# The last 96 hidden columns and the gate column computed with x stationary, turned by a transposing DMA

## The chip, the cores and the metric

The kernel runs on one core of one Trainium2 chip. It is a program for five engines that run side by side and meet only at semaphores: TensorE (PE, matmuls; PEld is its loading of weights), VectorE (DVE), ScalarE (ACT), GpSimd (POOL), and SyncE (SP), which here only issues DMAs. The metric is the device time of one execution in microseconds (us); the median of three runs is given.

## The reference

With x of 2048 tokens by 512, in bf16:

```python
g = sigmoid((x * gate_w).sum(-1))                 # one gate per token
a = linear_attention(x, wqkv, w_phi) @ wo         # 32 heads of 16
b = relu(x @ w1) @ w2                             # w1: 512 x 1376
return g * a + (1 - g) * b
```

In the attention branch q and k are projected per head by `w_phi`; the softmax of the result and the softmax of its negative, side by side, are the features. k features and v make one 32 x 16 matrix per head (`kv`), and each token's output is its q features times `kv`, divided by its q features times the sum of the k features. Nothing is causal: all of k and v must be done before the first output.

## The kernel before

**Tiling.** Tokens are taken in four chunks of 512 (index c or a) and 16 tiles of 128 (index m). x is kept transposed in `XT` (features on the partitions). `W1` has 1376 columns in eleven tiles of 128 (index k); the last tile has only 96 (`KREM`), and the gate weights are loaded as column 1376 beside it, so that the gate logits come out of the same matmuls.

**The hidden layer.** For each chunk and column tile, `pe_h` (line 394) makes four matmuls over the 512 features, with W1's columns stationary and 512 tokens moving. The result has the hidden columns on the partitions and the tokens along the row, which is the layout that the second layer needs as its stationary operand. ACT's Relu (`rl{a}_{k}`, line 460) copies it from PSUM to `HT`. For the last column tile (k = 10) 97 partitions come out: 96 hidden columns and, on partition 96, the 512 gate logits of the chunk.

**The gate.** DVE clamps this one row (`gr`, line 464), a DMA writes it to a scratch tensor in DRAM (`g1`, line 435), and a second DMA reads it back so that each token is on a partition of its own (`g2`, line 438). ACT makes the exponential (`ge`) and adds one (`gp`), DVE takes the reciprocal (`go`): 1 - g is 1/(1 + e), and g is e/(1 + e). `EG` scales the attention branch (line 615), `OMG` the output (line 679).

**The attention branch.** `v` (line 480) and the projections `pr` (line 499, with `w_phi` folded into the weights first, `pe_fold`, line 372) run on PE between the hidden tiles; maximum, minimum, sum and reciprocal run on DVE, subtractions and scalings on POOL, exponentials on ACT. `kv` (line 560) gathers k features and v on PE. For q, a transposing DMA per tile turns the features (`tq`, line 582), `nd` (line 604) multiplies them with `kv`, DVE divides (`rd`, `o`), and a second transposing DMA turns the result (`to`, line 620).

**The output.** `b{m}` (line 625) multiplies a tile of `HT` with `W2`, `a{m}` (line 632) adds the turned attention output times `wo` into the same PSUM bank; ACT scales and copies (`oe`), and a store follows (`st`).

**What sets the order.** Each engine's whole order of work is written out by hand in `ORDER` at the top, one list of step names per engine. An engine goes through its list strictly in order and waits at each step for the semaphores of what the step needs. SP's list is therefore also the order in which its DMAs are issued. PSUM has eight banks; the hidden tiles take turns in banks 3, 4 and 5 (`HB`), and a bank is free again when what is in `freed` is done, for the last column tile the Relu and the clamp.

Of the kernel before, what the change touches and what calls it, by code (L numbers as in the profile page):

```python
# [5 lines left out]
ACT = mybir.ActivationFunctionType  # L6
# [9 lines left out]

ORDER = {
# [4 lines left out]
    ),  # L22
    "pool": (
# [125 lines left out]
def bass_gated_mix__linear_kernel_hedgehog__dense_activation_relu__prompt_kernel(  # L149
# [13 lines left out]
    S, D = x2.shape  # L163
# [24 lines left out]
    with ExitStack() as es:  # L188
        E = es.enter_context

        def sb(name, shape, dt):
            return E(nc.sbuf_tensor(name, shape, dt))
# [31 lines left out]
        ROWM = sb("ROWM", [P, GH], I32)  # L224
        GB = sb("GB", [P, P], FP32)
        MK = sb("MK", [P, GH], FP32)
        GROW = sb("GROW", [P, 2, 512], FP32)
        GL = sb("GL", [P, NT], FP32)
        EG = sb("EG", [P, NT], FP32)
        EP = sb("EP", [P, NT], FP32)  # L230
        OMG = sb("OMG", [P, NT], FP32)
        PS = E(nc.psum_tensor("PS", [P, 8, 512], FP32))
        GSCR = nc.dram_tensor("gate_scratch", [S], FP32)
        EPS = 8 * 512

        def ap(t, row, off, dims):
            return bass.AP(tensor=t, offset=off, ap=[[row, P]] + [list(d) for d in dims])

        def psap(off, dims):
            return ap(PS, EPS, off, dims)  # L240
# [8 lines left out]
            boost=700.0)  # L249
        add("ones", "pool", lambda q: q.memset(  # L250
            ap(VS, NT * NG * GZ, GV, [[GZ, NT * NG], [1, 1]]), 1.0), dur=0.7, boost=-1e4)
        XN = FT[:, NF - 2, :].rearrange("p (m d) -> p m d", d=D)
        one = nc.const_aps.tensor(1.0, (P, 1), BF16).tensor
        ones_w, ones_m = (bass.AP(tensor=one, offset=0, ap=[[1, P], [0, n]]) for n in (P, 512))
# [26 lines left out]
        def chunk(c):  # L281
            return slice(c * 512, (c + 1) * 512)
# [109 lines left out]
        w1of = {k: (() if k < 4 else ("w1b",) if k < 8 else ("w1c",)) for k in range(KT)}  # L392

        def pe_h(q, c, k, b):
            m = P if k < KT - 1 else KREM + 1
            for j in range(ND):
                last = q.matmul(PS[0:m, b, :], W1[:, j, k * P:k * P + m], XT[:, j, chunk(c)],  # L397
                                start=(j == 0), stop=(j == ND - 1))
            return last

        def pe_h_first(q, j, c0, c1):
# [30 lines left out]
        def gate(c):  # L432

            s4 = slice(4 * c, 4 * c + 4)
            add(f"g1_{c}", "sp", lambda q, c=c: q.dma_start(out=GSCR[chunk(c)].rearrange("(o n) -> o n", o=1),
                                                             in_=GROW[KREM:KREM + 1, c % 2, :]),
                (f"gr{c}",), dur=0.1, lat=2.0, dma=True)
            add(f"g2_{c}", "sp", lambda q, c=c, s4=s4: q.dma_start(
                out=GL[:, s4], in_=GSCR[chunk(c)].rearrange("(m p) -> p m", p=P),
                allow_slow_non_contiguous=True),  # L440
                (f"g1_{c}",), dur=0.2, lat=3.0, dma=True)
            add(f"ge{c}", "act", lambda q, s4=s4: q.activation(EG[:, s4], GL[:, s4], ACT.Exp), (f"g2_{c}",), dur=0.22)
            add(f"gp{c}", "act", lambda q, s4=s4: q.activation(EP[:, s4], EG[:, s4], ACT.Copy, bias=1.0), (f"ge{c}",),
                dur=0.2)
            add(f"go{c}", "dve", lambda q, s4=s4: q.reciprocal(OMG[:, s4], EP[:, s4]), (f"gp{c}",), dur=0.15)

        for n, (kind, a, k) in enumerate(units):
            b = GB4[n] if n < 4 else HB[(n - 4) % len(HB)]
            if kind == "h":
                rows = P if k < KT - 1 else KREM  # L450
                halved = n < 4
                deps = [*xof[a], *w1of[k], prev, *freed[b]]
                if k == KT - 1:
                    deps.append("gw")
                add(f"h{a}_{k}", "pe", lambda q, a=a, k=k, b=b, h=halved:
                    pe_h_rest(q, k, (3 if k < 2 else 2) * P, 4 * P, k > 1) if h else pe_h(q, a, k, b),
                    deps, dur=(0.22 if k < 2 else 0.44) if halved else 0.87,
                    boost=8000.0 if n < 3 else 0.0)
                prev = f"h{a}_{k}"
                add(f"rl{a}_{k}", "act", lambda q, a=a, k=k, b=b, rows=rows: q.activation(  # L460
                    HT[0:rows, k, chunk(a)], PS[0:rows, b, :], ACT.Relu), (prev,), dur=0.6, boost=RL)
                freed[b] = (f"rl{a}_{k}",)
                if k == KT - 1:
                    add(f"gr{a}", "dve", lambda q, a=a, b=b: q.tensor_scalar(
                        GROW[KREM:KREM + 1, a % 2, :], PS[KREM:KREM + 1, b, :], GATE_LIMIT, -GATE_LIMIT,
                        ALU.min, ALU.max), (prev, f"rl{a}_{k}", f"g1_{a - 2}" if a > 1 else None), dur=0.69, boost=500.0)
                    freed[b] += (f"gr{a}",)
                    gate(a)
            else:
                deps = ["wqT", *wbd, prev, *freed[b]]  # L470
                add(f"f{a}_{k}", "pe", lambda q, a=a, k=k, b=b: pe_fold(q, a, k, b), deps, dur=0.24, boost=1000.0)
                prev = f"f{a}_{k}"
                evict(f"fe{a}_{k}", FE, WP[:, a, k, :], b, (prev,), boost=1000.0)
                freed[b] = (f"fe{a}_{k}",)
# [32 lines left out]
        for jn, (kind, tiles) in enumerate(jobs):  # L507
# [61 lines left out]
            else:  # L569
# [29 lines left out]
                for m in tiles:  # L599
# [39 lines left out]
                    if m == NT - 1:  # L639

                        hb = (ab, 0)
                        cols = [slice(0, 352), slice(352, D)]
                        last_b = f"b{m}"

                        def pe_bh(q, m=m, hb=hb, cols=cols):
                            for b, cs in zip(hb, cols):
                                for k in range(KT):
                                    r = P if k < KT - 1 else KREM
                                    last = q.matmul(PS[:, b, 0:cs.stop - cs.start], HT[0:r, k, m * P:(m + 1) * P], W2[0:r, k, cs],  # L649
                                                    start=(k == 0), stop=False)  # L650
                            return last

                        g.add(last_b, "pe", pe_bh, ("w2a", "w2b", *(f"rl{m // 4}_{k}" for k in range(KT)), *war,
                                                    f"ev_{J}"), dur=2.42)
                        for h2 in range(2):
                            b, cs = hb[h2], cols[h2]

                            def pe_ah(q, m=m, b=b, cs=cs):
                                for t in range(ND):
                                    last = q.matmul(PS[:, b, 0:cs.stop - cs.start], OT[:, m % NOT, t, :], WO[:, t, cs],  # L660
                                                    start=False, stop=(t == ND - 1))
                                return last

                            add(f"a{m}_{h2}", "pe", pe_ah, (last_b, "wo", f"to{m}", f"a{m}_0" if h2 else None), dur=0.44)
                            need = (f"a{m}_{h2}", f"go{m // 4}", f"st{m - NOS}")
                            if h2 == 0:
                                add(f"oe{m}_0", "act", lambda q, m=m, b=b, cs=cs: q.activation(
                                    OSB[:, m % NOS, cs], PS[:, b, 0:cs.stop - cs.start], ACT.Copy, scale=OMG[:, m:m + 1]), need, dur=0.45)
                            else:
                                add(f"oe{m}_1", "dve", lambda q, m=m, b=b, cs=cs: q.tensor_scalar(  # L670
                                    OSB[:, m % NOS, cs], PS[:, b, 0:cs.stop - cs.start], OMG[:, m:m + 1], None, ALU.mult), need,
                                    dur=0.4)
                            add(f"st{m}_{h2}", ("act", "sp")[h2], lambda q, m=m, cs=cs: q.dma_start(
                                out=o2[m * P:(m + 1) * P, cs], in_=OSB[:, m % NOS, cs]), (f"oe{m}_{h2}",), dur=0.5,
                                lat=1.5, dma=True)
                        continue
                    g.add(f"b{m}", "pe", pe_b, ("w2a", "w2b", *(f"rl{m // 4}_{k}" for k in range(KT)), *war), dur=2.38)
                    add(f"a{m}", "pe", pe_a, (f"b{m}", "wo", f"to{m}"), dur=0.87)
                    add(f"oe{m}", "act", lambda q, m=m, ab=ab: q.activation(  # L679
                        OSB[:, m % NOS, :], PS[:, ab, :], ACT.Copy, scale=OMG[:, m:m + 1]),  # L680
# [66 lines left out]
```

## Time and profile before

| | |
|---|---|
| Time, median of 3 runs | 151.53 us (151.14, 151.53, 152.31) |
| The profiled execution: span | 150.2 us, 2515 instructions |
| Median less that span | 1.33 us |
| PE / DVE / ACT / POOL busy | 145.2 / 113.4 / 92.2 / 109.4 us |
| Clamp of the gate row (DVE, 1x512) | 4 times 697 ns |
| Tail Relu (ACT, 96x512) | 4 times 599 ns |
| Transposing DMA of an attention tile (128x512) | 16, median 2.4 us from issue to landing |
| Gate read back from DRAM | 4, median 3.7 us from issue to landing |

All other times come from the one profiled execution, whose first instruction of the program is at 0 and whose last ends at 150.2. For that execution only the span is given; what a run takes beyond it lies around the program's instructions. The page gives the busy time of each engine, the span in 40 slices of 3.75 us each (a digit is the busy share in tenths), the chain of work that ended last, the groups of instructions by line, and the DMA issues. A group row ends with busy time, mean duration of one, and idle time before. Matmuls overlap one another, so the mean duration of one (379 ns for 512 columns) is longer than the distance from one to the next (216 ns), which is read from the chain: four in 0.86 us.

### The profile page before, as it was taken

To read this page: it belongs to the slowest core of one execution; us is meant where nothing else is said; L and a number is where in the kernel's file an instruction comes from. 1 tells how busy PE (TensorE), PEld (TensorE's weight loads), DVE (VectorE), ACT (ScalarE), POOL (GpSimd) and SP (SyncE) were. 2 spreads that over 40 slices of the span, in tenths; PEclk is the share of its full clock that TensorE was granted. 3 is DMA by queue.
4 is the path that set the end of the run, shared out by engine and by line. 5 is a ranking of instruction groups with operands and counts; after the bars stand their busy time and mean duration, and the time that the engine had idled before them with its cause. 6 is when DMAs were issued, how large, how long until landed. Compare 5 with 4: busy or idle time off the path is not lost.

```text
span 150.2 us, 2515 instructions
## 1 busy us (share of the span) xinstructions
PE 145.2 (97%) x944; PEld 74.2 (49%) x961; DVE 113.4 (76%) x168; ACT 92.2 (61%) x127; POOL 109.4 (73%) x71
## 2 busy tenths in 40 slices
PE   7899999999999999999999999999999999999992
PEld 3664444445554465445444545445444454454461
DVE  2433666999899949979999899999999969436301
ACT  3356769799969766698983937446546551310151
POOL 3000499999999999999999999998999791330000
PEclk9999999999999999999999999999999999999999
DMA  4999995000005602300000230476698774986251
GB/s 146 280 179 233 213 203 108 0 0 0 7 1 132 218 4 66 103 0 0 4 0 0 56 86 18 92 175 140 174 110 173 179 209 105 109 212 140 64 162 53
DMA packets 46307, 15.59 MB, mean 104 GB/s; under 512 B 39796, under 2 KB 46292, under 8 KB 46296
## 3 DMA queue, kind: packets, MB, share of 16 engines
q1 hardware_dynamic: 43560, 12.99, 42.0%
q10 hardware_dynamic: 2736, 2.45, 5.1%
q8 instruction: 7, 0.11, 0.4%
q14 instruction: 4, 0.03, 0.1%
HBM read 4.42 MB, written 2.11 MB: 43 GB/s over the span
## 4 chain that ended last, share of the span: by engine, by line
PE 93%; DMA 3%; issue 1%; ACT 1%; SPq 1%; DVE 0%
PE PS L628 24%; PE PS L397 23%; PE PS L502 18%; PE PS L482 9%; PE PS L634 9%; PE PS L563 3%; PE PS L606 3%; DMA W<-in_B_w_dram 3%; PE PS L649 2%; PE PS L374 1%; ACT HT L460 1%; PE PS L403 1%; PE PS L660 1%; SPq L272 1%; PE PS L409 0%
## 5 line engine op out<-in xcount | busy, mean ns | idle before, releaser
L542 POOL TENSOR_TENSOR TS<-PB,MX 128x1024 bf16<-128x1024 bf16 (+1 forms) x18 | 30.9, 1723 | 14.9 <-DVE MX L533 14.9
L397 PE MATMUL PS<-XT,W 128*128 128x512 bf16 (+1 forms) x156 | 38.3, 379 | 0.2
L628 PE MATMUL PS<-W,HT 128*128 128x512 bf16 (+1 forms) x160 | 37.5, 379 | 0.3
L549 DVE TENSOR_REDUCE ZB<-FT 128x128 f32<-128x2048 bf16 (+1 forms) x18 | 36.6, 2031 | 1.0 <-ACT FT L547 1.0
L547 ACT ACTIVATE FT<-TS 128x2048 bf16<-128x2048 bf16 (+1 forms) x18 | 30.9, 1718 | 7.7 <-POOL TS L542 7.5
L542 POOL TENSOR_TENSOR TS<-MN,PB 128x1024 bf16<-128x1024 bf16 (+1 forms) x18 | 30.9, 1724 | 0.8 <-DVE MN L535 0.8
L502 PE MATMUL PS<-WP,XT 128*128 128x512 bf16 x124 | 30.0, 379 | 0.2
L556 POOL TENSOR_TENSOR FT<-FT,SC 128x2048 bf16<-128x2048 bf16 (+1 forms) x9 | 29.5, 3290 | 0.0
L460 ACT ACTIVATE HT<-PS 128x512 bf16<-128x512 f32 (+1 forms) x44 | 24.7, 597 | 5.8 <-PE PS L397 4.9
L628 PEld LDWEIGHTS PS<-W,HT 128*128 128x128 bf16 (+1 forms) x165 | 15.5, 98 | 17.1
L533 DVE TENSOR_REDUCE MX<-PB 128x64 bf16<-128x1024 bf16 (+1 forms) x18 | 19.5, 1085 | 5.8 <-ACT PB L529 5.7
L397 PEld LDWEIGHTS PS<-XT,W 128*128 128x128 bf16 (+1 forms) x160 | 15.6, 101 | 16.5
L679 ACT ACTIVATE OSB<-PS,OMG 128x512 bf16<-128x512 f32 x15 | 10.2, 687 | 20.3 <-PE PS L634 20.3
L535 DVE TENSOR_REDUCE MN<-PB 128x64 bf16<-128x1024 bf16 (+1 forms) x18 | 19.3, 1084 | 2.3 <-ACT PB L529 2.3
L529 ACT ACTIVATE PB<-PS 128x1024 bf16<-128x1024 f32 (+1 forms) x18 | 16.7, 927 | 6.7 <-PE PS L502 3.8
L502 PEld LDWEIGHTS PS<-WP,XT 128*128 128x128 bf16 x128 | 12.1, 98 | 13.9 <-DVE WP L344 0.4
L579 POOL TENSOR_TENSOR FT<-FT,SR 128x1024 bf16<-128x1024 bf16 (+1 forms) x9 | 15.6, 1739 | 0.7
L482 PE MATMUL PS<-WV,XT 128*128 128x512 bf16 x62 | 16.0, 379 | 0.1
L634 PE MATMUL PS<-WO,OT 128*128 128x512 bf16 x58 | 14.2, 378 | 0.1
L615 DVE SCALAR_TENSOR_TENSOR OTM<-PS,EG,RD 128x256 bf16<-128x256 f32 x32 | 13.8, 463 | 0.2
L613 DVE RECIPROCAL RD<-PS 128x16 f32<-128x16 f32 x32 | 6.5, 235 | 9.0 <-PE PS L606 8.8
L491 ACT ACTIVATE VS<-PS 128x512 bf16<-128x512 f32 x16 | 9.6, 603 | 4.8 <-PE PS L482 4.7
(50 smaller groups left out, 97.8 us busy)
## 6 DMA issues: line engine op xcount, KB each, us to landing
out_dram<-OSB ACTq DMA_DIRECT2D x15, 128.0 KB, 2.1
W<-in_B_w_dram SPq DMA_DIRECT2D x1, 1280.0 KB, 6.7
W<-in_B_w_dram SPq DMA_DIRECT2D x1, 512.0 KB, 5.6
WV<-in_A_wqkv_dram SPq DMA_DIRECT2D x1, 512.0 KB, 4.7
WO<-in_A_wo_dram SPq DMA_DIRECT2D x1, 512.0 KB, 4.7
FT<-in_A_x_dram SPq DMA_DIRECT2D x3, 128.0 KB, 4.0
W<-in_B_w_dram SPq DMA_DIRECT2D x1, 352.0 KB, 3.9
W<-in_B_w_dram ACTq DMA_DIRECT2D x2, 128.0 KB, 3.7
```

Of the source, the lines that this page charges most:

```text
L397: last = q.matmul(PS[0:m, b, :], W1[:, j, k * P:k * P + m], XT[:, j, chunk(c)], start=(j == 0), stop=(j == ND - 1))
L460: add(f"rl{a}_{k}", "act", lambda q, a=a, k=k, b=b, rows=rows: q.activation(HT[0:rows, k, chunk(a)], PS[0:rows, b, :], ACT.Relu), (prev,), ...
L482: last = q.matmul(PS[:, 2, :], XT[:, j, m * P:(m + 1) * P], WV[:, j, :], start=(j == 0), stop=(j == ND - 1))
L502: last = q.matmul(PS[:, n, :], XT[:, j, m * P:(m + 1) * P], WP[:, s, j, :], start=(j == 0), stop=(j == ND - 1))
L533: add(f"mx_{J}", "dve", lambda q, sl=sl, w=w, i=pbg: q.tensor_reduce(MX[:, sl, 0:w * H], i, AX.X, ALU.max), (f"ev_{J}", old("t1")), dur=0. ...
L535: add(f"mn_{J}", "dve", lambda q, sl=sl, w=w, i=pbg: q.tensor_reduce(MN[:, sl, 0:w * H], i, AX.X, ALU.min), (f"ev_{J}", old("t2")), dur=0. ...
L542: add(f"{tn}_{J}", "pool", lambda q, o3=o3, a3=a3, b3=b3: q.tensor_tensor(o3, a3, b3, ALU.subtract), (f"{'mx' if sg == 0 else 'mn'}_{J}", ...
L547: add(f"ex_{J}", "act", lambda q, fs=fs, ts=ts, w=w: q.activation(FT[:, fs, 0:w * F], TS[:, ts, 0:w * F], ACT.Exp), (f"t1_{J}", f"t2_{J}", ...
L549: add(f"sm_{J}", "dve", lambda q, fs=fs, sl=sl, w=w: q.tensor_reduce(ZB[:, sl, 0:2 * w * H], FT[:, fs, 0:w * F].rearrange("p (g d) -> p g ...
L556: add(f"nm_{J}", "pool", lambda q, f3=f3, sl=sl, w=w: q.tensor_tensor(f3, f3, SC[:, sl, 0:2 * w * H].unsqueeze(2).to_broadcast([P, 2 * w * ...
L628: last = q.matmul(PS[:, ab, :], HT[0:r, k, m * P:(m + 1) * P], W2[0:r, k, :], start=(k == 0), stop=False)
L634: last = q.matmul(PS[:, ab, :], OT[:, m % NOT, t, :], WO[:, t, :], start=False, stop=(t == ND - 1))
```

## The change

For the last column tile the operands change places. `pe_h_tail` makes four groups of four matmuls per chunk: 128 tokens of x stationary, the 97 columns of W1 (with the gate column) moving. The result has tokens on the partitions and, for each of the four token tiles, 97 values along the row. The Relu copies 4 x 96 of these to a new tile `HR`, whose rows are padded to 128 columns with zeros once at the start (`hpad`, on POOL). A transposing DMA `hx{a}` on SP's queue turns `HR` into the place of the tail in `HT`; the output step `b{m}` now waits for it. The gate logits are already one token per partition: the clamp reads four values per partition from PSUM straight into `GL`, and `g1`, `g2`, `GROW` and the DRAM scratch are gone.

```diff
     "sp": (
-        "... x3 gw g1_1 g2_1 w2a g1_0 g1_2 w2b wo g2_0 tq0 tq1 "
-        "g1_3 to0 tq2 tq3 to1 tq4 tq5 to2 to3 tq6 to4 tq7 g2_3 to5 g2_2 tq8 to6 ..."
+        "... x3 gw w2a w2b wo hx0 hx1 hx2 tq0 tq1 "
+        "hx3 to0 tq2 tq3 to1 tq4 tq5 to2 to3 tq6 to4 tq7 to5 tq8 to6 ..."
     "pool": (
-        "iota_r iota_i iota_c ones t1_k0 ..."
+        "iota_r iota_i iota_c ones hpad t1_k0 ..."
...
-        GROW = sb("GROW", [P, 2, 512], FP32)
+        HR = sb("HR", [P, 2, 4, P], BF16)
...
-        GSCR = nc.dram_tensor("gate_scratch", [S], FP32)
...
+        add("hpad", "pool", lambda q: q.memset(HR[:, :, :, KREM:P], 0.0), dur=0.6, boost=-1e4)
...
+        def pe_h_tail(q, c, b):
+            m = KREM + 1
+            for n in range(4):
+                for j in range(ND):
+                    last = q.matmul(PS[:, b, n * m:(n + 1) * m], XT[:, j, c * 512 + n * P:c * 512 + (n + 1) * P],
+                                    W1[:, j, (KT - 1) * P:(KT - 1) * P + m], start=(j == 0), stop=(j == ND - 1))
+            return last
...
-            add(f"g1_{c}", "sp", ...)
-            add(f"g2_{c}", "sp", ...)
-            add(f"ge{c}", "act", lambda q, s4=s4: q.activation(EG[:, s4], GL[:, s4], ACT.Exp), (f"g2_{c}",), dur=0.22)
+            add(f"ge{c}", "act", lambda q, s4=s4: q.activation(EG[:, s4], GL[:, s4], ACT.Exp), (f"gr{c}",), dur=0.22)
...
+                    add(f"h{a}_{k}", "pe", lambda q, a=a, b=b: pe_h_tail(q, a, b), deps, dur=0.69)
+                    prev = f"h{a}_{k}"
+                    hrow = psap(b * 512, [[KREM + 1, 4], [1, KREM]])
+                    add(f"rl{a}_{k}", "act", lambda q, a=a, i=hrow: q.activation(
+                        HR[:, a % 2, :, 0:KREM], i, ACT.Relu), (prev, f"hx{a - 2}" if a > 1 else None), dur=0.6, boost=RL)
+                    add(f"hx{a}", "sp", lambda q, a=a: q.dma_start_transpose(
+                        out=HT[:, KT - 1, chunk(a)].rearrange("p (n t) -> p n t", t=P),
+                        in_=HR[:, a % 2, :, :].rearrange("p n k -> p (n k)")),
+                        (f"rl{a}_{k}", "hpad"), dur=1.2, lat=1.6, dma=True)
+                    add(f"gr{a}", "dve", lambda q, a=a, b=b: q.tensor_scalar(
+                        GL[:, 4 * a:4 * a + 4], psap(b * 512 + KREM, [[KREM + 1, 4]]), GATE_LIMIT, -GATE_LIMIT,
+                        ALU.min, ALU.max), (prev, f"rl{a}_{k}"), dur=0.2, boost=500.0)
+                    freed[b] = (f"rl{a}_{k}", f"gr{a}")
...
-                    g.add(f"b{m}", "pe", pe_b, ("w2a", "w2b", *(f"rl{m // 4}_{k}" for k in range(KT)), *war), dur=2.38)
+                    g.add(f"b{m}", "pe", pe_b, ("w2a", "w2b", *(f"rl{m // 4}_{k}" for k in range(KT - 1)), f"hx{m // 4}", *war), dur=2.38)
```

The orders of PE, ACT and DVE stay as they were.

More of the change, by code (lines that the diff above doesn't have):

```diff
@@ L394, in pe_h @@
         def pe_h(q, c, k, b):
-            m = P if k < KT - 1 else KREM + 1
             for j in range(ND):
-                last = q.matmul(PS[0:m, b, :], W1[:, j, k * P:k * P + m], XT[:, j, chunk(c)],
+                last = q.matmul(PS[:, b, :], W1[:, j, k * P:(k + 1) * P], XT[:, j, chunk(c)],
                                 start=(j == 0), stop=(j == ND - 1))
+            return last
[5 more added lines that the diff above has]
+                                    W1[:, j, (KT - 1) * P:(KT - 1) * P + m], start=(j == 0), stop=(j == ND - 1))
             return last
@@ L434, in gate @@
             s4 = slice(4 * c, 4 * c + 4)
[L435 to L441, printed above, removed]
-            add(f"ge{c}", "act", lambda q, s4=s4: q.activation(EG[:, s4], GL[:, s4], ACT.Exp), (f"g2_{c}",), dur=0.22)
+            add(f"ge{c}", "act", lambda q, s4=s4: q.activation(EG[:, s4], GL[:, s4], ACT.Exp), (f"gr{c}",), dur=0.22)
             add(f"gp{c}", "act", lambda q, s4=s4: q.activation(EP[:, s4], EG[:, s4], ACT.Copy, bias=1.0), (f"ge{c}",),
@@ L449, in bass_gated_mix__linear_kernel_hedgehog__dense_activation_relu__prompt_kernel @@
             if kind == "h":
-                rows = P if k < KT - 1 else KREM
                 halved = n < 4
@@ L454, in bass_gated_mix__linear_kernel_hedgehog__dense_activation_relu__prompt_kernel @@
                     deps.append("gw")
+                    add(f"h{a}_{k}", "pe", lambda q, a=a, b=b: pe_h_tail(q, a, b), deps, dur=0.69)
[11 more added lines that the diff above has]
+                    freed[b] = (f"rl{a}_{k}", f"gr{a}")
+                    gate(a)
+                    continue
                 add(f"h{a}_{k}", "pe", lambda q, a=a, k=k, b=b, h=halved:
@@ L459, in bass_gated_mix__linear_kernel_hedgehog__dense_activation_relu__prompt_kernel @@
                 prev = f"h{a}_{k}"
-                add(f"rl{a}_{k}", "act", lambda q, a=a, k=k, b=b, rows=rows: q.activation(
-                    HT[0:rows, k, chunk(a)], PS[0:rows, b, :], ACT.Relu), (prev,), dur=0.6, boost=RL)
+                add(f"rl{a}_{k}", "act", lambda q, a=a, k=k, b=b: q.activation(
+                    HT[:, k, chunk(a)], PS[:, b, :], ACT.Relu), (prev,), dur=0.6, boost=RL)
                 freed[b] = (f"rl{a}_{k}",)
[L463 to L468, printed above, removed]
             else:
@@ L651, in pe_bh @@
                             return last
-                        g.add(last_b, "pe", pe_bh, ("w2a", "w2b", *(f"rl{m // 4}_{k}" for k in range(KT)), *war,
+                        g.add(last_b, "pe", pe_bh, ("w2a", "w2b", *(f"rl{m // 4}_{k}" for k in range(KT - 1)), f"hx{m // 4}", *war,
                                                     f"ev_{J}"), dur=2.42)
```

6 rows, old and new, of the table ORDER are left out of this document.

## The prediction

> **What bounds the kernel now.** I read the page first: the busy shares, the slices, and the shares of the chain that ended last.
>
> ```profile
> PE 145.2 (97%) x944; PEld 74.2 (49%) x961; DVE 113.4 (76%) x168; ACT 92.2 (61%) x127; POOL 109.4 (73%) x71
> ...
> PE   7899999999999999999999999999999999999992
> ...
> PE 93%; DMA 3%; issue 1%; ACT 1%; SPq 1%; DVE 0%
> ```
>
> TensorE is busy in every slice after the first, and 93% of the chain is PE. A busy PE could still hide waits, so the waits came second: who stood idle, and for whom.
>
> ```profile
> PE PS L403 <- DMA W<-in_B_w_dram: 0.4, 1, 0.4
> ...
> PEld PS L634 <- DMA OT<-OTM: 0.5, 2, 0.3
> ...
> PEld PS L606 <- DMA PHQ<-FT: 0.2, 1, 0.2
> ```
>
> The first row is at the start, at 5.7 us. After 13 us no matmul waits for anything; only weight loads do, 0.7 us in three places, while the matmuls ahead of them still run. So the time is the sum of what PE issues: shortening PE is the only thing that shortens the kernel, and the most that can come of it is what PE is spared, less what new waits take back.
>
> Third, the price of one matmul. The mean durations in the groups are latencies; matmuls overlap. The spacing is read from the chain in order of time (start, us, what):
>
> ```profile
> 37.05 0.26 PE PS L563 x8
> 37.31 0.88 PE PS L397 x4
> ...
> 56.37 0.22 PE PS L374 x4
> ...
> 85.00 0.88 PE PS L397 x4
> ```
>
> The rows with 0.88 are the tail groups that the change replaces (h0_10, h3_10): 4 matmuls with 97 stationary and 512 moving columns. Row L563 has 8 matmuls with 65 moving columns, each with a weight load of its own: 0.26/8 = 32 ns. Row L374 has 4 with 128 moving columns, again a load each: 0.22/4 = 55 ns.
>
> **The change part by part.**
>
> *PE.* Removed: four tail groups. Two stand at 0.88; the other two lie in rows with full tiles (40.18 0.86 x4; 52.78 2.59 x12), 0.86 each: 3.48 in all. Added: per chunk 16 matmuls with 97 moving columns, each with a load of 128 columns. No row has 97. The bounds are 32 ns (65 columns) and 55 ns (128 columns). On a line between them 97 columns cost 32 + 23 x 32/63 = 44 ns; 160 columns, in the last four matmuls of the chain (a15_1, 0.28/4 = 70 ns), lie on the line too. I take 43 to 44: 16 x 43.5 = 0.70 per group, 2.78 for four, a gain of 0.70 us. The ends are 16 x 32 = 0.51 (gain 1.43) and 16 x 55 = 0.88 (loss 0.04). That four matmuls add into the same columns one after the other costs nothing at 128 columns (row L409, 12 in 0.69, 57 ns each); closer spacing isn't shown.
>
> Row against rule: by the Trainium skill (TensorE: Matmul & The Clock Gate, Back-to-back issue gap) a stream of load and matmul pairs is paced by both, about 81 ns at 128 columns. An estimate by that page is 16 x 81 = 1.30 per group, 1.7 us more in all and 153.2. The trace doesn't agree: its pairs at 128 columns stand at 55 ns.
>
> *ACT.* Relu of the tail reads 4 x 96 columns instead of 512. Rows: 599 ns for 96x512, 554 for 352 columns; so about 560, 0.04 less. ACT waits for PE; nothing on the path.
>
> *DVE.* The clamp gr goes from 1x512 (697 ns) to 128x4; the nearest row is the reciprocal of 128x4 (149 ns). Four times 0.55 less, bounds 0 and 0.7. DVE isn't the bound, but gr3 (90.39, 0.70) stands ahead of rd0 and o0, which feed the first transpose of the output stage, so that stage starts about 0.55 earlier on DVE. It also waited 2.23 us at gr2 for the tail Relu, now earlier with PE.
>
> *SyncE queue.* Removed: eight small DMAs (issue 0.23 to 0.59 each). Added: four transposes of 128x512, the shape of OT<-OTM: issue 1.19 to 2.54, median 1.21; landing 2.3 to 4.8, median 2.4. The queue in order of time:
>
> ```profile
> 22.78 0.58 SPq L272 DMA_DIRECT2D W<-in_gate_w_dram  x1
> 43.84 0.32 SPq L435 DMA_DIRECT2D gate_scratch<-GROW  x1
> ...
> 84.41 2.60 SPq L582 DMA_TRANSPOSE PHQ<-FT  x2
> 91.12 0.25 SPq L435 DMA_DIRECT2D gate_scratch<-GROW  x1
> 92.43 2.54 SPq L620 DMA_TRANSPOSE OT<-OTM  x1
> ```
>
> hx0, hx1 and hx2 wait for Relus that end at about 40, 41.9 and 56.0; behind them only tq0 waits, ready at 84.4. The first reader is b0 at 87.9, 30 us after hx2 lands. hx3 waits for the Relu that ends at 87.4, while SP is free from 87.0 to 91.1: it leaves SP at 88.7, or 90.0 with the longest issue, ahead of to0, which now issues at 92.43 and can at about 91.9 once gr3 is short. Its first reader is the fourth chunk's first output tile, b13, at 132.7. So no wait is added on the path: cost 0, and if the cover between 87.0 and 91.9 went, see the second rival.
>
> *Loads.* w2a, w2b and wo no longer stand between gate DMAs: they go out right behind the gate column, at 23.4 instead of 45.4 to 57.5. Nothing is behind them until hx0, and the DMA slices from 26 to 41 us read 0. The gate column is ahead in the queue and needed at 37.3; even with the 6.7 us of the large load before it it lands in time. Cost 0, and no gain, as b0 is the first reader.
>
> *POOL.* hpad, 256 elements of each partition: the 128-element memset took 0.67, so 0.2 to 1.4, in a gap of 14.9 us ahead of the first subtraction. Cost 0.
>
> *Gate on ACT.* One wait goes, 2.6 us for the logits of chunk 3 at 113.3. PE did not wait there; gain 0.
>
> *What is late next.* Three weight loads already wait for transposes, so PE's lead of 0.7 could be lost there:
>
> ```profile
> 97.85 0.39 PEld L606 LDWEIGHTS PS<-KVN,PHQ 128*128 128x128 bf16 x8 [0.24 <-DMA PHQ<-FT]
> ...
> 114.01 0.69 PEld L634 LDWEIGHTS PS<-WO,OT 128*128 128x128 bf16 x4 [0.18 <-DMA OT<-OTM]
> ...
> 131.36 0.56 PEld L634 LDWEIGHTS PS<-WO,OT 128*128 128x128 bf16 x4 [0.31 <-DMA OT<-OTM]
> ```
>
> The first is tq2, queued behind to0, which moves 0.55 earlier with gr3: 0 to 0.2 lost. The second is to5, which was queued behind a scattered gate load (issued 109.04, landed 113.3) that is gone: 0. The third is to10, which follows nd10 through DVE's reciprocal; those reciprocals waited for PE seven times, 8.8 us in all, so it moves with PE: 0 to 0.3. I take 0 of these, and 0.7 as the worst, since a wait for work that is no later than before can take back no more than the gain.
>
> **The sum.** 3.48 - 2.78 = 0.70 off PE, all on the path, nothing added to it. The profiled execution's span is 150.2, so the changed one's is 149.5. The median of the three runs, 151.53, is 1.33 above that span, time around it and scatter (151.14 to 152.31); I leave it as it is: 151.53 - 0.70 = 150.8, 0.5% less. About 1% (1.5 us) is what a measurement of this kernel can tell from no change, so this is no change by that bound.
>
> **Rivals.**
> 1. *Weight loads set the pace.* Place: the 64 new pairs. The load row says 98 ns for 128 columns; if a load isn't hidden behind a matmul of 44 ns, a group costs 16 x 98 = 1.57, 0.70 more than now, 2.8 in all: 154.3, slower. It turns at 0.87/16 = 54 ns a pair, and passes 1% at 54 + 1500/64 = 78 ns. For it: old tail matmuls had 379 ns each to hide a load. Against it: row L563, 32 ns with the same load. By the Trainium skill's rule cited above it would be a milder form of the same. Chance 0.07.
> 2. *The transposes crowd the queue.* Place: SP between tq1 and to0. If hx3 leaves SP after 91.9, or holds up what is queued behind it by as much as the longest landing exceeds the median (2.4), tq2 and nd2 are late by up to that: 150.8 + 2.4 = 153.2. For it: to0 and to10 have shown such long ones. Against: 3 us of slack. Chance 0.06.
> 3. *The gain is given back* at tq2 and to10: 151.1 to 151.6. For: they are already late. Chance 0.22.
> 4. *More than forecast*: pairs at 32 ns, 150.1, or a stage that DVE's 2.2 us and the lighter queue speed up though PE shows no idle time there: 149.9. Against: the rows at 55 ns. Chance 0.07.
>
> **How the numbers follow.** Forecast (150.4 to 151.1): 0.58. Under 150.0 (faster by over 1%): 0.06, out of case 4. Over 153.05 (slower by over 1%): most of cases 1 and 2, 0.12. The rest, 0.82, is within 1%. The range 150.0 to 152.3 holds the forecast, case 3, a loss of 0.04 at 55 ns a pair, and the scatter of the runs above these; outside are case 1, case 2 and part of case 4.
>
> **What would show it.** The four tail groups at about 0.70 in the chain instead of 0.86 to 0.88; the tail's pairs at 43 to 44 ns; the clamp under 0.2 us; transposes of the tail issued near 40, 42, 56 and 87 us; b0 starting some 0.7 earlier than 87.9; no PE wait for them. Wrong would be pairs at over 54 ns, or a wait over 0.5 of PE or PEld for PHQ or OT near 97 or 131 us.

## The result, and the profile after

The changed kernel takes 151.19 us, the median of 22 runs (150.54 to 152.10); the kernel before, run beside it, 151.96 (22 runs, 151.14 to 152.43). The ratio is 0.9958, with a 95% interval of 0.9944 to 0.9972. That is 0.64 us or 0.4% less: a small gain, and within the 1% that counts as no change here. The forecast, 150.8 against 151.53, was a ratio of 0.995. The kernel before has a median 0.43 above that of the three runs from which the forecast started; the ratio is free of this.

The profiled execution of the changed kernel has a span of 148.9 us. Its page, first the busy time of each engine with its share and its number of instructions, then the slices, then the shares of the chain:

```profile
PE 144.6 (97%) x992; PEld 75.3 (51%) x1009; DVE 111.0 (74%) x168; ACT 91.9 (62%) x127; POOL 109.6 (74%) x72
...
PE   7999999999999999999999999999999999999992
...
PE 96%; ACT 1%; issue 1%; DVE 0%
```

PE bounds the kernel as before. The busy time of PE fell by 0.6 only, although 48 more matmuls are counted: more matmuls, but shorter ones. What they cost is read from the chain in order of time (start, us, what):

```profile
36.68 0.26 PE PS L571 x8
36.93 0.69 PE PS L404 x16
...
39.61 0.69 PE PS L404 x16
...
53.77 0.69 PE PS L404 x16
...
84.10 0.69 PE PS L404 x16
...
86.78 2.38 PE PS L636 x11
```

The four rows with L404 are the tail groups. Each takes 0.69 us instead of 0.86 to 0.88, and its 16 matmuls start 43.3 ns apart. Row L636 is `b0`: it starts at 86.78. The groups of the changed kernel (busy, mean ns of one, idle time before) show the new steps on the other engines:

```profile
L404 PE MATMUL PS<-W,XT 128*128 128x97 bf16 x64 | 3.4, 207 | 0.0
L404 PEld LDWEIGHTS PS<-W,XT 128*128 128x128 bf16 x64 | 3.1, 98 | 0.5
...
L457 ACT ACTIVATE HR<-PS 128x384 bf16<-128x384 f32 x4 | 2.0, 508 | 0.1
...
L463 DVE TENSOR_SCALAR GL<-PS 128x4 f32<-128x4 f32 x4 | 0.6, 138 | 2.0 <-ACT HR L457 2.0
```

A load still lasts 98 ns, more than twice the distance of the pairs, so loads overlap one another as well as the matmuls. The Relu takes 508 ns, the clamp 138 instead of 697. SP's queue in order of time (start, us until the next one can go, what):

```profile
22.93 1.22 SPq L272 DMA_DIRECT2D W<-in_B_w_dram  x2
24.19 0.51 SPq L272 DMA_DIRECT2D WO<-in_A_wo_dram  x1
39.57 16.64 SPq L459 DMA_TRANSPOSE HT<-HR  x3
84.01 3.23 SPq L590 DMA_TRANSPOSE PHQ<-FT  x2
87.29 1.27 SPq L459 DMA_TRANSPOSE HT<-HR  x1
90.76 1.19 SPq L628 DMA_TRANSPOSE OT<-OTM  x1
91.99 2.66 SPq L590 DMA_TRANSPOSE PHQ<-FT  x2
```

`w2a`, `w2b` and `wo` go out at 23 to 24 us. `hx0` to `hx2` are the row with x3 (16.64 us are mostly waits for the Relus); `hx3` is issued at 87.29 and `to0` at 90.76, 1.67 us earlier than before.

**Where the time went.** By the ends of the matmuls in the two traces, PE's last one ends 1.03 us earlier (147.31 before, 146.28 after). The four tail groups give 0.19, 0.17, 0.17 and 0.18 of it, 0.71 together. Another 0.38 stands in the first 12 us, 0.3 of it in the first 7: before, the first W1 tile came 0.39 late for PE (the row L403 of the prediction), this time it didn't. The changed kernel's loads at the start are the same as before, and a second profile of it, shown below, waits there again; so the 0.38 is taken as scatter of the two executions. The remaining -0.06 was lost at `a3`, which waited for `to3`.

One more wait is new, and a weight load shows it; in this execution it costs the matmuls nothing. The timeline of PEld in the changed kernel (idle time before in brackets):

```profile
141.93 0.57 PEld L642 LDWEIGHTS PS<-WO,OT 128*128 128x128 bf16 x4 [0.29 <-DMA OT<-OTM]
```

This is `a14` waiting for the transpose `to14`. It landed 3.9 us after its issue, where the median of the 16 is 2.4.

### The profile page after: what moved, and what is told of

Same layout as the page of the kernel before. It is cut to its first block, busy times and chain, and to the rows that moved or that the text cites. A ratio compares the mean times of both kernels' runs of the same rounds, so it can differ in the third digit from the quotient of the medians.

```text
span 148.9 us, 2614 instructions
## 1 busy us (share of the span) xinstructions
PE 144.6 (97%) x992; PEld 75.3 (51%) x1009; DVE 111.0 (74%) x168; ACT 91.9 (62%) x127; POOL 109.6 (74%) x72
## 4 chain that ended last, share of the span: by engine, by line
PE 96%; ACT 1%; issue 1%; DVE 0%
PE PS L636 24%; PE PS L396 21%; PE PS L510 18%; PE PS L490 9%; PE PS L642 9%; PE PS L571 3%; PE PS L614 3%; PE PS L404 2%; PE PS L258 2%; PE PS L657 2%; PE PS L410 1%; PE PS L374 1%; PE PS L350 1%; ACT HT L474 1%; PE PS L668 1%
## 5 line engine op out<-in xcount | busy, mean ns | idle before, releaser
L550 POOL TENSOR_TENSOR TS<-PB,MX 128x1024 bf16<-128x1024 bf16 (+1 forms) x18 | 30.9, 1722 | 14.3 <-DVE MX L541 14.3
L636 PE MATMUL PS<-W,HT 128*128 128x512 bf16 (+1 forms) x160 | 37.5, 379 | 0.3
L396 PE MATMUL PS<-XT,W 128*128 128x512 bf16 x141 | 34.3, 379 | 0.2
L474 ACT ACTIVATE HT<-PS 128x512 bf16<-128x512 f32 x40 | 22.6, 597 | 5.5 <-PE PS L396 4.6
L636 PEld LDWEIGHTS PS<-W,HT 128*128 128x128 bf16 (+1 forms) x165 | 15.5, 98 | 17.1
L396 PEld LDWEIGHTS PS<-XT,W 128*128 128x128 bf16 x144 | 13.8, 98 | 15.3
L642 PE MATMUL PS<-WO,OT 128*128 128x512 bf16 x58 | 14.3, 379 | 0.1
L623 DVE SCALAR_TENSOR_TENSOR OTM<-PS,EG,RD 128x256 bf16<-128x256 f32 x32 | 13.8, 463 | 0.4 <-DVE RD L621 0.2
```

The lines of the kernel that those rows point to most:

```text
L396: last = q.matmul(PS[:, b, :], W1[:, j, k * P:(k + 1) * P], XT[:, j, chunk(c)], start=(j == 0), stop=(j == ND - 1))
L474: add(f"rl{a}_{k}", "act", lambda q, a=a, k=k, b=b: q.activation(HT[:, k, chunk(a)], PS[:, b, :], ACT.Relu), (prev,), dur=0.6, boost=RL)
L550: add(f"{tn}_{J}", "pool", lambda q, o3=o3, a3=a3, b3=b3: q.tensor_tensor(o3, a3, b3, ALU.subtract), (f"{'mx' if sg == 0 else 'mn'}_{J}", ...
L636: last = q.matmul(PS[:, ab, :], HT[0:r, k, m * P:(m + 1) * P], W2[0:r, k, :], start=(k == 0), stop=False)
L642: last = q.matmul(PS[:, ab, :], OT[:, m % NOT, t, :], WO[:, t, :], start=False, stop=(t == ND - 1))
```

## The experiments

The main theory, theory 1 in the expectations: PE issues 0.7 us less in the four tail groups, this alone is the gain, and the rest of the change (clamp, gate on chip, queue, earlier loads) neither gives nor costs anything that shows. Against it stand that the loads pace short pairs, that part of the gain comes from the queue or the gate and not from PE, that the earlier loads matter, and that the four new transposes come close to holding up the queue. Ratios are against the kernel before on the same chip.

### E1: the new form without its saving

From the changed kernel; the moving part is 128 columns of W1 instead of 97, of which 31 are not used.

```diff
-            m = KREM + 1
+            m = P
...
-                                    W1[:, j, (KT - 1) * P:(KT - 1) * P + m], ...
+                                    W1[:, j, DFF + 1 - m:DFF + 1], ...
...
```

The places in PSUM that the Relu and the clamp read move along with it.

> The changed kernel, with 128 instead of 97 moving columns in each tail matmul (the 31 columns ahead of the tail are computed once more and thrown away); all else as changed. Theory 1, the time is the sum of what PE issues: a pair costs 55 ns as in the folding rows, a group 0.89 instead of 0.69, so 0.8 us more than the changed kernel, that is the time of before within 0.2 us (ratio to before 0.999 to 1.001). Theory 2, the gain comes from the gate path, the shorter clamp and the lighter DMA queue: it stays, ratio 0.996.

Measured: ratio 1.0027 (1.0004 to 1.0049), median 152.52 against 151.88. The tail groups in the chain of E1:

```profile
37.12 0.91 PE PS L404 x16
...
54.38 0.91 PE PS L404 x16
...
84.92 0.91 PE PS L404 x16
```

16 pairs in 0.91 are 57 ns each, 4 x 0.91 = 3.64 in all, 0.16 above the 3.48 of the kernel before and 0.88 above the changed kernel. With clamp, gate, queue and loads all as changed, the gain is gone and the kernel is 0.3% slower than before: 1.05 us more than the changed kernel by the two ratios, 0.88 by PE. So the gain depends on PE's columns. The ratio lies above the 1.001 that was expected; PE's 0.16 is less than half of the 0.41 us above the kernel before, but lies within its interval (0.06 to 0.74 us). I had put the pair at 55 ns from row L374; 57, as in row L409, is right.

### E2: the saving without the new form

From the kernel before; only 416 of the 512 tokens move through the tail group, so that it lasts about as long as the new one. The last hidden columns (1280 to 1375) and the gate logits of the last 96 tokens of each chunk are left out.

```diff
-            m = P if k < KT - 1 else KREM + 1
+            m, t = (P, 512) if k < KT - 1 else (KREM + 1, 416)
...
-                last = q.matmul(PS[0:m, b, :], W1[...], XT[:, j, chunk(c)],
+                last = q.matmul(PS[0:m, b, 0:t], W1[...], XT[:, j, c * 512:c * 512 + t],
```

> The kernel before, with only 416 of the 512 tokens moving in each tail group, so that hidden columns 1280 to 1375 and the gate are not computed for the last 96 tokens of each chunk; gate path, clamp and queue as before. Theory 1: a tail group costs 4 x 176 ns = 0.70 instead of 0.87, the same saving on PE as the change, so 0.6 to 0.7 us less than before, ratio 0.995 to 0.997. Theory 2: ratio 1.000.

Measured: ratio 0.9958 (0.9932 to 0.9983), median 151.31. The groups in the chain of E2:

```profile
37.43 0.72 PE PS L397 x4
...
40.14 0.70 PE PS L397 x4
...
84.65 0.72 PE PS L397 x4
```

PE's steps are 0.16 shorter four times, 0.64 in all, and the time falls by as much, 0.42%. The old clamp, the trip of the gate through DRAM, the wait for it on ACT and the loads between are all still there. So a shorter tail on PE by itself gives a gain of the changed kernel's size, as far as the interval tells (0.26 to 1.03 us). Together with E1 this is the cause.

### E3: how far down the pairs go, and what binds next

From the changed kernel with 33 moving columns: the last 32 hidden columns and the gate. 64 hidden columns are left out and stand as zeros.

```diff
-            m = KREM + 1
+            m = 33
...
-                    hrow = psap(b * 512, [[KREM + 1, 4], [1, KREM]])
+                    hrow = psap(b * 512, [[33, 4], [1, 32]])
...
```

> The changed kernel with 33 moving columns in each tail matmul: 32 hidden columns and the gate, the other 64 hidden columns of the tail left out as zeros. It measures what paces a pair of load and matmul when the matmul is short. If the moving columns alone set it (0.417 ns a column and some 2.5 ns), a pair costs 16 ns, a group 0.26, and the kernel is 1.7 us faster than the changed one (ratio to before 0.984 to 0.986). If the weight load of 128 columns sets it, as the 32 ns of the rows with 65 and 68 columns would allow, a pair costs 32 ns, a group 0.52, and 0.7 us come off (ratio 0.991 to 0.992). By the Trainium skill (TensorE: Matmul & The Clock Gate, the section on 56 and 53.3 ns) matmuls never start closer than about 25 ns; an estimate by that is 0.40 a group and 1.2 us (ratio 0.988).

Measured: ratio 0.9937 (0.9915 to 0.9958), median 151.04. The timeline of PE in E3 (start, us, and the next start below it):

```profile
37.67 0.55 PE L404 MATMUL PS<-W,XT 128*128 128x33 bf16 x16
38.07 0.42 PE L571 MATMUL PS<-VS,FT 128*128 128x65 bf16 x8
```

The next group starts 0.40 after the tail group, 25 ns a pair; the matmuls of a tail group start 25.2 ns apart. Each pair still has a load of 128 columns whose row says 96 ns. So the loads do not pace pairs down to 25 ns, and the first rival of the prediction falls. The measured value is neither of the two that I had put up, 16 by columns alone and 32 as at 65 columns. By the Trainium skill (TensorE: Matmul & The Clock Gate, "Wait — 56ns, not 53.3ns?") starts of matmuls never stand closer than about 25 ns; the measured 25.2 agrees.

PE is spared another 1.2 us here, but only some 0.3 us come off. The waits of E3 (who, for whom: us, how often, the longest):

```profile
PEld PS L510 <- issue: 0.7, 1, 0.7
PEld PS L571 <- POOL FT L564: 0.6, 1, 0.6
...
PE PS L510 <- ACT EG L442: 0.3, 1, 0.3
```

None of these is in the changed kernel. 0.43 is lost at the first projection of q, 0.32 at the last `kv`, which waits for POOL's scaling, and 0.13 at the first `nd`; the chain of E3 runs through POOL for 42% of it, where that of the changed kernel has 96% PE:

```profile
PE 49%; POOL 42%; issue 5%; ACT 1%; DVE 1%; POOLq 0%
```

Once PE is 1.2 us ahead, the attention branch's POOL and ACT are in the way.

### E4 and E8: PE's change alone, with the gate through DRAM

Both start from the changed kernel and put back a trip of the logits through DRAM, a 1x512 operation on DVE in the place of the old clamp, and the old places of the loads in SP's list.

```diff
-        "... gw w2a w2b wo hx0 hx1 hx2 tq0 tq1 hx3 to0 tq2 tq3 to1 tq4 tq5 to2 to3 tq6 to4 tq7 to5 tq8 ..."
+        "... gw hx0 hx1 g1_1 g2_1 w2a g1_0 hx2 g1_2 w2b wo g2_0 tq0 tq1 hx3 g1_3 to0 tq2 ... tq7 g2_3 to5 g2_2 tq8 ..."
...
+            add(f"g1_{c}", "sp", lambda q, c=c, s4=s4: q.dma_start(
+                out=GSCR[chunk(c)].rearrange("(m p) -> p m", p=P), in_=GLR[:, s4], ...   # E4
+                out=GSCR[chunk(c)].rearrange("(p m) -> p m", p=P), in_=GLR[:, s4]), ...  # E8
...
-            add(f"ge{c}", "act", ..., (f"gr{c}",), dur=0.22)
+            add(f"ge{c}", "act", ..., (f"g2_{c}",), dur=0.22)
```

> The changed kernel with all but its PE part put back: the logits go through DRAM again (two DMAs per chunk at their old places in the queue), each clamp is followed by a dummy clamp of 1x512, and the loads of W2 and WO stand behind the gate DMAs again. Theory 1: the gain stays, ratio 0.995 to 0.997, at most 0.3 us lost at weight loads that wait for OT near 114 and 131 us. Theory 2: ratio 1.000.

Measured: ratio 1.1492 (1.1459 to 1.1524), median 174.75. This experiment does not do what I meant. The waits of E4:

```profile
ACT EG L451 <- DMA GL<-gate_scratch: 15.8, 2, 14.3
...
PE PS L399 <- ACT HT L485: 13.2, 1, 13.2
```

The logits lie one token per partition now, so writing them in token order makes 4-byte pieces. This write took 12.2 us from issue to landing (median of 4, from 9.7 to 14.9). ACT stood 14.3 us at the exponential of a gate, its Relus stood behind it, and PE waited 13.2 us for one of them. The TensorE clock that was granted to its runs is 0.94 of the full one, where the kernel before has 1.00, so the 22.9 us are not all waiting. E4 shows only what a late gate costs on an engine that works strictly in order.

E8 writes 16 bytes per partition in one piece instead (the order in the scratch is free, as it is read back in the same one): 2.3 us from issue to landing (median of 4, from 1.4 to 7.2), 2.8 for the way back.

> The run that put the gate path back once more, but with the logits written to DRAM and read back four neighbouring values per partition at a time (16 bytes) instead of scattered by 4 bytes, so that no DMA of it takes some 10 us; the dummy clamp of 1x512 and the old places in the queue stay. Theory 1 (PE alone): the gain of the change stays, ratio 0.995 to 0.998, and no wait of ACT's exponential for the logits that reaches PE. Theory 2 (the gain is that of the gate path, the clamp and the queue): ratio 1.000 or more.

Measured: ratio 1.0004 (0.9984 to 1.0025), median 151.98, beside the changed kernel itself (E9) at 0.9972 (0.9949 to 0.9996), median 151.52. So the saving on PE didn't come through, against theory 1. The waits of E8:

```profile
ACT EG L451 <- DMA GL<-gate_scratch: 1.4, 2, 1.1
...
PEld PS L399 <- ACT HT L485: 0.5, 1, 0.5
...
PEld PS L501 <- ACT VS L510: 0.4, 1, 0.4
```

The tail groups are as short as in the changed kernel, but ACT waits 1.4 us for gates, its copies behind are late, and PE loses 0.16 at `h3_3` and 0.11 at `v10`. In E2 PE was about as early, with the old trip, and lost nothing; its trip is another one (a row instead of 128 pieces, four transposes fewer on the queue). So theory 1 needs a second half: the saving is PE's, and a gate trip of E8's kind takes back some 0.3 us of it. The changed kernel with the old kind of trip was not run. That the intervals of E8 and E9 overlap leaves the size open.

### E5: the loads alone

From the kernel before; only the place of the three loads in SP's list is changed.

```diff
-        "... gw g1_1 g2_1 w2a g1_0 g1_2 w2b wo g2_0 tq0 tq1 "
+        "... gw w2a w2b wo g1_1 g2_1 g1_0 g1_2 g2_0 tq0 tq1 "
```

> The kernel before, with nothing changed but SP's order: the loads of W2 and WO go out right behind the gate column, ahead of the gate DMAs. Theory 1: no change, ratio 0.999 to 1.001. Theory 2 (the queue matters): part of the gain, ratio 0.997 or 0.998.

Measured: ratio 1.0006 (0.9984 to 1.0028), median 151.96. The earlier loads give and cost nothing that shows.

### E6, E7 and E10: how much cover the new transposes have

From the changed kernel; three (E6, and again E10) or six (E7) further transposes of `HR` stand behind `hx3`, into a tile that nothing reads.

```diff
-        "hx3 to0 tq2 ..."
+        "hx3 hy0 hy1 hy2 to0 tq2 ..."
...
+                    for y in range(3 if a == 3 else 0):
+                        add(f"hy{y}", "sp", lambda q, y=y: q.dma_start_transpose(
+                            out=HY[:, y, :, :], in_=HR[:, 1, :, :].rearrange("p n k -> p (n k)")), ...
```

> The changed kernel with three more transposes of the same size issued right behind hx3, into a buffer that nobody reads. They hold SP from 87.3 to about 92.4, so to0 goes out 1.6 us late and tq2 lands at about 96.4 instead of 94.8; PE needs it at 97.0. Theory 1: still covered, the time of the changed kernel within 0.3 us, ratio 0.995 to 0.998. Rival (the transposes crowd the queue): the 1.6 us come through, ratio 1.006.

> The same with six more transposes: SP is held until about 96.2, to0 is 5.4 us late, tq2 lands at about 100.2, 3.2 us after PE needs it. Theory 1 with the cover used up: 2 to 3.5 us more than the changed kernel, ratio 1.010 to 1.020, and a wait of PE's weight load for PHQ of 2 to 3.5 us near 97 us. If the queue's place did not matter at all: ratio 0.996.

Measured: three take 1.0003 (0.9976 to 1.0030), six 1.0281 (1.0240 to 1.0322). SP's queue in E6:

```profile
89.03 3.89 SPq L465 DMA_TRANSPOSE HY<-HR  x3
92.97 1.27 SPq L633 DMA_TRANSPOSE OT<-OTM  x1
```

and in E7, with its waits in the fence behind:

```profile
88.78 8.09 SPq L465 DMA_TRANSPOSE HY<-HR  x6
96.91 1.26 SPq L633 DMA_TRANSPOSE OT<-OTM  x1
```

```profile
PE PS L647 <- DMA OT<-OTM: 2.5, 1, 2.5
...
PEld PS L619 <- DMA PHQ<-FT: 1.1, 1, 1.1
```

A transpose holds the queue for 1.3 us, so three push `to0` from 90.8 to 93.0 and six to 96.9. In E6 `tq2` lands 0.45 ahead of its use, and PE waits for neither it nor `to0`; it loses 0.11 at `a3`. In E7 `to0` lands at 99.33, while `a0` wants it at about 96.7: PE loses 3.7 us in all, 2.65 of it at `a0`. I had reckoned with `tq2` alone and overlooked `a0`, which stands ahead of it. By the ratios six more transposes cost 4.9 us over the changed kernel, where 2 to 3.5 were expected; the run with the profile took 155.48, 4.3 above the changed kernel's median of 151.19, and three of the six runs took 156.7 to 157.1. What these three lose beyond PE's 3.7 is not shown.

E6's time was above what its trace gives reason for, and its interval was too wide to tell; so it was run again beside the unaltered changed kernel.

> Three more transposes behind hx3, as before. In its first profile tq2 landed only 0.4 us and to3 0.1 us before PE needed them. If that cover holds in most runs, ratio within 0.002 of the changed kernel beside it. If the slack of 0.4 us is less than landings vary by from run to run, it stays 0.003 to 0.005 slower than the changed kernel, and a profile shows a weight load waiting for PHQ or OT.

> The changed kernel itself, as a control on the same chip: ratio 0.994 to 0.998.

Measured: E10 0.9990 (0.9963 to 1.0017), median 151.54; the changed kernel 0.9972 (0.9949 to 0.9996), median 151.52. The time of the three transposes is not resolved: the two medians agree, but the median span of E10 is 150.0 and that of E9 149.65. And this execution of E10 has waits:

```profile
PEld PS L619 <- DMA PHQ<-FT: 1.0, 1, 1.0
PEld PS L647 <- DMA OT<-OTM: 0.7, 1, 0.7
PE PS L619 <- DMA PHQ<-FT: 0.5, 1, 0.5
```

Here `tq2` landed 0.47 after its use. With three more the slack is 0.45 at one time and -0.47 at the next: the cover behind `hx3` is three transposes, some 4 us of queue, and the change itself takes one.

### E11 and E12: why to3 and to14 are late

In the unaltered changed kernel, profiled three times, the weight loads of `a3` or `a14` wait for their transposes. Neither was late before. The waits of PE's loads for `OT` in E9, and behind it those of E12, the third profile:

```profile
PEld PS L642 <- DMA OT<-OTM: 0.6, 1, 0.6
```

```profile
PEld PS L642 <- DMA OT<-OTM: 0.6, 2, 0.4
```

Against groups that wait for nothing, PE loses 0.06 in the first, 0.35 in the second and 0.36 in the third execution, at `a3` and `a14` together. The DMA views of a window show a candidate (packets, MB and share of a queue; transposes with their median landing). Before, 138 to 141 us:

```profile
OT<-OTM SPq DMA_TRANSPOSE x2, 2.3
```

After, the same window:

```profile
q8 instruction: 1, 0.02, 2.9%
...
OT<-OTM SPq DMA_TRANSPOSE x2, 3.3
```

The queue q8 carries instructions: blocks of 16 KB. Before there are seven, at 13.8, 38.1, 56.2, 74.0, 93.1, 111.2 and 128.2 us; after, with 96 more instructions on PE, there are eight, at 13.3, 36.5, 52.9, 66.9, 84.8, 103.2, 122.4 and 139.0. The one at 103.2 falls on `to3`, the one at 139.0 on `to14`. Before, those at 93.1 and 128.2 fell on `to0` and `to10`, which have the longest issue (2.54) and the longest landing (4.8) of the `OT` transposes of that trace. E11 moves the blocks: from the changed kernel with the warming matmuls at the start cut into 24 of 128 columns instead of 6 of 512, which is the same work in more instructions.

```diff
-    WARM = (6 * (512,),)
+    WARM = (24 * (128,),)
```

> The changed kernel, with the six idle warm-up matmuls of 512 columns at the start cut into 24 of 128 columns: the same columns, but 36 more PE instructions (18 matmuls, 18 loads) ahead of everything else. Theory: the page of PE instructions that is fetched at 139 us, and delays the transpose to14 that PE then waits for, is fetched some 2.3 us earlier (36 instructions at 256 per 16.6 us), beside to13, which has 3 us of slack. Then a14 and a3 wait for nothing, to14 lands 2.4 us after its issue instead of 3.9, and 0.1 to 0.35 us come off the changed kernel: 0.001 to 0.002 less than it in the ratio. If the delay of to14 has another cause (its place in the queue), it stays where it is.

> The changed kernel once more beside the run with the finer warm-up: ratio 0.994 to 0.998; to14 lands late again and PE's weight load waits 0.2 to 0.6 us for OT near 142 us.

Measured: E11 0.9955 (0.9937 to 0.9974), median 151.20; E12 0.9967 (0.9947 to 0.9988), median 151.52. The times don't part them. In the trace of E11 the block at 103.2 now comes at 100.6, `to3` lands 1.46 ahead of its use, and `a3` takes 0.86 again: as expected. But the last block came at 139.1, not at 136.7, and `to14` stayed slow (3.5 us, landing 0.64 ahead of its use). Over the kernel before, E11 and the three profiles of the changed kernel, a block began between issue and landing of 13 of the 80 `OT` transposes: they landed after 3.4 to 4.8 us, and of the other 67 all but four within 3.1. So a late landing goes with a block, with and without the change, and moves with it where the block moves. What sets the time of a block is not settled: the instruction count alone, by which I reckoned, does not.

## Why the prediction was right

**The bound.** Right. PE is 96% of the chain, and what PE issues less is what the time lost (E1, E2).

**PE, 43 to 44 ns a pair.** Right: 43.3 ns, and 0.71 us off the four groups where 0.70 stood in the sum. The line through 65, 128 and 160 columns was the right reading. The row against the rule: 57 ns at 128 columns in E1, each with its own load, where the Trainium skill (TensorE: Matmul & The Clock Gate, Back-to-back issue gap) has about 81; the measurement decides, and the first rival falls with it.

**ACT.** The Relu was mis-sized, 560 against 508 ns; nothing hangs on it.

**DVE.** 138 ns against 149. The clamp went from 697, and `to0` left at 90.8, 1.1 us ahead of the 91.9 that was reckoned with the short clamp. In these two executions PE itself is 1.1 us earlier there (`b0` starts at 86.78 instead of 87.87), 0.38 of it by the scatter at the start.

**SP.** Right in place and cost: transposes at 39.6 and 87.3, `hx3` off the queue at 88.6 (88.7 was forecast), no wait near 97. The second rival did not come, and E6, E7 and E10 give its price: nothing sure up to three more, 4.9 us over the changed kernel with six more.

**Loads and POOL.** Right. E5 gives 1.0006 for the loads; the memset took 635 ns, within 0.2 to 1.4.

**The gate on ACT, gain 0.** Right for the kernel before: E2 keeps the old trip and has a gain of the full size. Incomplete for the changed one, where a trip of E8's kind costs PE some 0.3 us: leaving out the trip gives no gain of its own, but a trip of that kind would have taken part of it back.

**What is late next.** This step failed in its places. All three that it named got better: by the transposes' events and the time at which PE is ready, `tq2` now lands 2.2 us ahead of its use instead of 0.3, `to5` and `to10` 2.5. For `to5` the reason given, the gate load ahead of it, does not hold: E2 and E5 keep that load, and there `to5` lands after 2.6 and 2.4 us instead of 4.2. In the kernel before, the block of instructions at 111.2 fell on `to5`; in E2 and E5 it comes at 113.0 and 113.6 and falls on `to6`, which lands after 4.2. Two that the prediction did not name, `to3` and `to14`, became late, by 0.06 to 0.36 us of PE in three executions. I looked for what was late already, and not for where the blocks of instructions fall in the changed kernel. The third rival, the gain given back, came in this small form, inside the forecast's range.

**Time around the span left as it is.** Off by 0.3. Over all runs the time less the span has a median of 1.56 us before and 1.88 after; the eleven kernels of the study fall into two groups, 1.5 to 1.6 (before, E2, E5, E6) and 1.8 to 1.9 (after and the rest). The median span fell from 150.4 to 149.5, more than the time did. Some 0.2 of it is no work: in the kernel before the span ends with SP's last semaphore instruction, 2.84 us after PE's last matmul, and in the changed kernel that one comes after 2.60, with those of the other engines. The rest isn't settled. Ends of matmuls (0.71 less the 0.06 to 0.36 lost) are the better measure here than spans.

**The sum.** 0.4% against 0.5%. It is right because its large term was priced by the spacing in the chain. That 0.64 comes so near to 0.70 is partly luck: the waits at `to3` and `to14`, which the sum put at 0, take back 0.06 to 0.36, and the interval of the gain is 0.43 to 0.85 us.

## What to carry to other kernels

Price short matmuls by their spacing in the chain and not by the mean duration in the groups: here pairs stand 43 ns apart whose matmul lasts 207 and whose load lasts 98. Where PE has no waits, what it issues less comes off the time, but only until the next engine is late: here 0.7 us came off almost whole, while of 1.2 more only 0.3 did. When a step goes onto a queue, take the slack of every reader behind it, the first in time above all, and of an in-order engine behind a late wait.

## What the runs showed of the hardware that I had not expected

**Very short pairs.** A matmul of 33 moving columns with a load of 128 columns of its own takes 25 ns (E3), one of 65 columns 32, of 97 columns 43, of 128 columns 57 (E1).

**Instructions beside transposes.** A 16 KB block of instructions that began while a transposing DMA of `OT` was under way went with a landing after 3.4 to 4.8 us, where the median of all is 2.4.

**The first microseconds.** The same kernel starts differently from one execution to the next. The timeline of PE in the changed kernel, and behind it in E9, which is the same kernel:

```profile
4.29 1.72 PE L410 MATMUL PS<-XT,W 128*128 128x128 bf16 x16
```

```profile
4.64 2.28 PE L410 MATMUL PS<-XT,W 128*128 128x128 bf16 x16 [0.17 <-DMA W<-in_B_w_dram]
```

The same 16 matmuls take 1.72 and 2.28 us, and start 0.35 apart. This scatter is as large as the whole gain, so the spans of two single profiles can't show the gain: the groups in the chain can, and the ratio over many runs.

**Small pieces to DRAM.** 512 values of 4 bytes, each in a place of its own, took 12.2 us from issue to landing in E4; the same number of values in pieces of 16 bytes took 2.3 in E8 (medians of four).
